# One VectorE maximum over two PSUM banks in every other burst of an attention kernel

## Chip, core and metric

The kernel runs on one core of one Trainium2 chip. The metric is the device time of one execution in microseconds (us); the time before is the median of three runs, 1784.49 us. Durations and waits come from one profiled execution of the kernel, which took 1784.4 us.

The engines named below are TensorE (PE in the profile; its weight loads are shown apart as PEld), VectorE (DVE), ScalarE (ACT), GpSimd (POOL) and SyncE (SP, which here only issues DMAs).

## What is computed

Two attention layers over one sequence (2048 rows, width 512, 32 heads of 16), mixed by a gate. Side A is full softmax attention. Side B is attention within four segments of 512 rows with a mask, plus a memory carried from segment to segment.

```python
def _A_ref(x, wqkv, wo):
    ...
    scores = jnp.einsum("bhqd,bhkd->bhqk", q, k) * scale
    p = _softmax(scores, axis=-1)
    o = jnp.einsum("bhqk,bhkd->bhqd", p, v)
    ...
def _B_ref(x, wq, wk, wv, wo, beta):
    ...
        logits = jnp.einsum("bhqd,bhkd->bhqk", qs, ks) * scale + mask
        p = _softmax(logits, axis=-1)
    ...
g = _sigmoid((x * gate_w).sum(-1, keepdims=True))
return g * a + (1 - g) * b
```

A softmax needs the maximum of each row of scores before the exponentials. The kernel takes these row maxima exactly, in a pass of its own, ahead of the scores whose exponentials it keeps. That pass is where the change lies.

## The kernel before

**Prologue** (about the first 300 us): projections of queries, keys and values for both sides, the memory of side B, and the maxima of the first 96 slots.

**Main loop.** The work is cut into 64 units: a side, a group of four heads, and a chunk of 512 query rows. A unit of side A has 64 slots, one of side B 10; a slot is one 512-column bank of scores. The loop `while n < nS or ...` (L1002 on) takes one score slot n and one maximum slot m = n + 96 per step, 2368 slots in all, so 2272 maximum slots (m from 96 to 2367) fall into the loop. The order of every queue is written out by hand: each engine executes its instructions in the order in which the loop emits them.

In one step the loop emits, in this order:

- `score_part(n)` (L726, L749): the score product on TensorE into one of three banks named `st`, then the exponential by ScalarE out of that bank into `p`.
- `max_part(m, ...)`: the product for the maxima on TensorE (L205, in `max_product`) into the bank `banks[m % 4]`, one of four PSUM banks of 512 fp32 columns named `sm0` to `sm3`; then VectorE takes the maxima of that bank. In a side-A slot this is one `tensor_reduce` of 512 columns (L226). In a side-B slot the bank holds one or two pieces (128 with 384 columns, 256 with 256, or one of 512), and each piece is a masked maximum (L238) and a short instruction that reads its accumulator. The first piece is emitted at once; a second piece waits in `rows_left` until `flush_rows()` in the next slot, after that slot's reduce.

Score products and maximum products alternate between the upper and the lower half of the array's rows, so the two of one slot run side by side.

A **burst** is three slots (`BURST = 3`). After the third slot of a burst the loop emits, on TensorE, one of three things: the products of the exponentials with the values (L783, `some_values`, 3 to 5 slots' worth, into the bank `ops`), or three products of the output projection (L895), or of a late query projection (L666). So TensorE's order in a burst is score, maximum, score, maximum, score, maximum, then this long block.

`maxs` lists whose maxima slot m takes. Slots of side B lie at m % 3 == 0, the first of a burst, so the second and third slot of a burst always belong to side A. When the last maximum of a unit is taken, `finish_max` reduces four key chunks to one (L183, VectorE), and the result travels through GpSimd, a transpose on TensorE and a DMA into rows of the query tile, 96 slots before the scores need it.

In the last 94 slots of scores no maxima remain; there the four banks serve the scores and the final products instead.

In the notes below M0 to M5 are the maximum products of six consecutive slots (m % 6 from 0 to 5), and R0 to R5 the reduces of these. A bank may be written again when the maximum out of it has ended: with four banks, product m waits for the reduce of slot m - 4.

Of the kernel before, what the change touches and what calls it, by code (L numbers as in the profile page):

```python
# [10 lines left out]
F32 = mybir.dt.float32  # L11
F32R = mybir.dt.float32r
AF = mybir.ActivationFunctionType
ALU = mybir.AluOpType
AX = mybir.AxisListType
# [7 lines left out]
CH = 512  # L23
# [24 lines left out]
def gated_mix(ctx, tc, x, xT, wqkv, a_wo, b_wq, b_wk, b_wv, b_wo, beta, gate_w, out):  # L48
    nc = tc.nc
# [129 lines left out]
    def finish_max(u):  # L179
        nm = pmt.pop(u)  # L180
        if u[0] == "A":
            pm, nm = nm, mp.tile([128, 4, 4], F32, tag="nm", name="nm")
            nc.vector.tensor_reduce(nm, pm, axis=AX.X, op=ALU.max, negate=True)  # L183

        ms = mp.tile([128, 2, 2, 2, 4], F32R, tag="ms", name="ms")
        nv = nm.rearrange("p (r h) s -> p r h s", r=2)
        nc.gpsimd.tensor_copy(ms[:, :, 0], nv)  # L187
        nc.gpsimd.tensor_sub(ms[:, :, 1], nv, ms[:, :, 0].bitcast(F32))
        return ms
# [14 lines left out]
    def max_product(ps, u, h, s, n0, n, k, k0=0):  # L204
        nc.tensor.matmul(ps[:, n0:n0 + n], rows(qt[u][:, :, s * 128:(s + 1) * 128], h, 48), rows(k[:, :, k0:k0 + n], h, 48),  # L205
                         start=True, stop=True)
# [3 lines left out]
    def flush_rows():  # L210
        while rows_left:
            rows_left.pop(0)()

    def max_part(m, bank):

        u, (r, i) = maxs[m]
        side, g, c = u
        if u not in pmt:
            pmt[u] = mp.tile([128, 4, 4] + [4] * (side == "A"), F32, tag="pm" + side, name="pm")
        pm = pmt[u]  # L220
        ps = bank()
        if side == "A":

            kc, s, h = i // 8, i % 8 // 2, 2 * r + i % 2
            max_product(ps, u, h, s, 0, CH, kt_[u, kc])
            nc.vector.tensor_reduce(pm[:, h, s, kc:kc + 1], ps, axis=AX.X, op=ALU.max)  # L226
            flush_rows()
        else:


            k = kt_[u, c]
            mine = [(2 * r + h, s, 128 * (s == 2) + 256 * (s == 1 and h), 128 * (s + 1))
                    for h, s in (((0, 0), (0, 2)), ((0, 1), (1, 1)), ((1, 0), (1, 2)), ((0, 3),), ((1, 3),))[i]]
            for h, s, n0, w in mine:
                max_product(ps, u, h, s, n0, w, k)
            flush_rows()
            for h, s, n0, w in mine:
                rows_left.append(lambda h=h, s=s, n0=n0, w=w: nc.vector.tensor_tensor_reduce(  # L238
                    out=tri["rest"][:, 0:w], in0=ps[:, n0:n0 + w], in1=tri["mask"][:, CH - w:], scale=-1.0, scalar=3.0e38,
                    op0=ALU.add, op1=ALU.min, accum_out=pm[:, h, s:s + 1]))  # L240
            rows_left.pop(0)()
        if m == last_max[u]:
            def finish():

                due = min(e for e in a_last if e >= last_max[u]) + LATE_T
                late.append((min(due, first[u] + LEAD - 12), u, finish_max(u)))
            todo.append((m + 1, finish))

    def run_todo(m):

        for e in [e for e in todo if e[0] <= m]:
            todo.remove(e)
            e[1]()

    def run_late(pool, tag, m):
        while us := [e for e in late if e[0] < m][:2]:
            for e in us:
                late.remove(e)
            transpose_max(us, pool, tag)
# [3 lines left out]
    def loads(m):  # L263

        m = min(m, len(maxs) - 1)
        while loaded[0] <= m:
            u, (r, i) = maxs[loaded[0]]
            if loaded[0] == first_max[u]:
                load_q(u)
            kc = u[2] if u[0] == "B" else i // 8  # L270
            if (u, kc) not in kt_:
                load_k(u, kc)
            loaded[0] += 1
# [3 lines left out]
    with ExitStack() as p0:  # L277
# [264 lines left out]
        def some_max():  # L542
            m = mnext[0]
            if m == LEAD:
                return
            loads(m + 3 + PRE)
            for i in range(4):
                max_part(m + i, lambda: me_sm.tile([128, CH], F32, tag="sm", name="sm"))
            run_todo(m + 3)
            mnext[0] += 4  # L550
            run_late(me_ps, "me", mnext[0])
# [51 lines left out]
    o_ps = ctx.enter_context(tc.tile_pool(name="o_ps", bufs=1, space=PSUM, reuse_waits="tile"))  # L603
    sm_ps = ctx.enter_context(tc.tile_pool(name="sm_ps", bufs=1, space=PSUM, reuse_waits="tile"))

    banks = [sm_ps.tile([128, CH], F32, name=f"sm{i}") for i in range(4)]

    ops = o_ps.tile([128, CH], F32, name="ops")

# [380 lines left out]
    def most():  # L990

        if not queue:
            return 0
        side = queue[0][1][0]
        left = SLOTS[side] - queue[0][2]
        over = 64 * (len(queue) - LOW) > (HIGH - LOW) * (left if side == "A" else 0)
        return ends[side].get(left, MOST + over)
# [3 lines left out]
    while n < nS or queue or beside or filled[0] < len(fill):  # L1001
        for f in beside.pop(n, []):  # L1002
            f()
        if n < nS:
            score_part(n)
        m = n + LEAD
        if m < nS:
            loads(m + PRE)

            max_part(m, lambda: banks[m % 4])  # L1010
        run_todo(m)
        if n >= nS or n % (2 * BURST if n in wide else BURST) == (2 * BURST if n in wide else BURST) - 1:
            taken = 0
            if shared:
                for _ in range(3):
                    shared.pop(0)()
            else:
                taken = some_values(n, 8 if n >= nS or n in wide else most())
            if n < 5:


                for i in range(4):
                    nc.tensor.matmul(ops[:, 128 * i:128 * i + 128], identf, identf, start=True, stop=True)
            if any(e[0] < m + 1 for e in late):
                run_late(st_ps, "st", m + 1)
            else:

                for _ in range(0 if n >= nS and queue else 4 if n not in wide else 11 - taken if taken < 8 else 0):
                    if filled[0] == len(fill) or fill[filled[0]][0] > n:
                        break  # L1030
                    fill[filled[0]][1]()
                    filled[0] += 1
        n += 1
# [18 lines left out]
def build():  # L1052
    import concourse.bacc as bacc
    nc = bacc.Bacc("TRN2", target_bir_lowering=False, num_devices=1)
    shapes = {"x": (S, D), "xT": (D, S), "wqkv": (D, 3 * D), "a_wo": (D, D), "b_wq": (D, D), "b_wk": (D, D),
              "b_wv": (D, D), "b_wo": (D, D), "beta": (H,), "gate_w": (D,)}
    args = [nc.dram_tensor(n, s, F32, kind="ExternalInput").ap() for n, s in shapes.items()]
    out = nc.dram_tensor("out", (S, D), F32, kind="ExternalOutput").ap()
    with tile.TileContext(nc) as tc:
        gated_mix(tc, *args, out)  # L1060
    return nc
# [23 lines left out]
```

## Time and profile before

| quantity | value |
|---|---|
| median of three runs | 1784.49 us (1784.37 to 1785.07) |
| the profiled execution | 1784.4 us |
| its span, first to last instruction | 1782.7 us |
| granted TensorE clock over the span | 1.000 |
| ScalarE busy | 1437.9 us, 81% of the span |
| GpSimd busy | 640.9 us, 36% of the span |

The profile's page gives, per engine, busy time and number of instructions, then the span in 40 slices, the DMA queues, the chain of work that ended last, and the costliest groups of instructions. A group's row reads: line, engine, operation, output tile and input tile, shapes, count, then busy time and mean duration of one. A row of the timeline reads: start in us, duration in us, engine, line, operation, tiles, shapes, count; in square brackets stands the idle time of the engine before it and what ended it. Two things matter in reading them. Matmuls are pipelined, so a busy TensorE row is not TensorE at its peak. And VectorE's durations overlap: the next instruction may start while the last one still drains, so the distance between starts is what an instruction costs when they follow closely.

### The profile page before, as it was taken

What the parts mean: (1) busy time and instruction counts of PE and PEld (TensorE: products, weight loads), DVE (VectorE), ACT (ScalarE), POOL (GpSimd) and SP (SyncE); (2) the same over time, 40 slices, a digit from 0 to 9 for tenths busy, and PEclk for the clock granted to TensorE, in tenths of its full rate; (3) what the DMA queues carried; (4) which work ended last, traced back from release to release, by engine and by line L of the source; (5) the groups of instructions that cost most, each with busy time, mean ns of one, the idle gap of its engine ahead of it and who ended that gap; (6) DMA issues with size and microseconds to landing.
All of it is one profiled execution on the core that took longest, in us unless ns stands there. A gap on an engine that the chain in (4) does not pass through costs nothing.

```text
span 1782.7 us, 40694 instructions
## 1 busy us (share of the span) xinstructions
PE 1773.5 (99%) x14945; PEld 912.4 (51%) x14945; DVE 1574.0 (88%) x3330; ACT 1437.9 (81%) x2754; POOL 640.9 (36%) x748
## 2 busy tenths in 40 slices
PE   9999999999999999999999999999999999999999
PEld 7887776444444444444444444444444444444444
DVE  4235777999999999999999999999999999999930
ACT  5455444888888888888888888888888888888884
POOL 3002222414161416443434343343434253435343
PEclk9999999999999999999999999999999999999999
DMA  7667555445463436544454544454545353544542
GB/s 227 219 226 249 189 195 192 132 103 140 108 169 107 134 116 180 147 136 135 134 134 128 146 127 146 128 146 115 157 106 156 115 142 116 147 119 140 144 161 61
DMA packets 142422, 261.55 MB, mean 147 GB/s; under 512 B 36328, under 2 KB 60680, under 8 KB 141712
## 3 DMA queue, kind: packets, MB, share of 16 engines
q1 hardware_dynamic: 140864, 257.69, 49.6%
q8 instruction: 119, 1.95, 0.5%
q0 software_dynamic: 1216, 1.14, 0.2%
q14 instruction: 79, 0.65, 0.1%
q10 hardware_dynamic: 144, 0.13, 0.0%
HBM read 174.39 MB, written 83.25 MB: 145 GB/s over the span
## 4 chain that ended last, share of the span: by engine, by line
PE 93%; DMA 2%; ACT 2%; DVE 1%; POOL 1%; issue 0%; SPq 0%; POOLq 0%; DVEq 0%; ACTq 0%
PE ops L783 33%; PE st L726 27%; PE sm L205 14%; PE pr L314 9%; PE ops L895 4%; PE ops L666 2%; PE sm L895 2%; DMA raw<-xT 1%; POOL mn L374 1%; PE num L496 1%; DMA qdA<-q 0%; DMA vs<-wqkv 0%; DMA qdB<-q 0%; DVE q L377 0%; ACT full L369 0%
## 5 line engine op out<-in xcount | busy, mean ns | idle before, releaser
L749 ACT ACTIVATE p<-st 128x512 f32<-128x512 f32 x2261 | 1189.4, 601 | 152.5 <-PE sm L205 108.6
L226 DVE TENSOR_REDUCE pm<-sm 128x1 f32<-128x512 f32 x2048 | 1280.8, 682 | 11.8 <-PE sm L205 11.6
L726 PE MATMUL st<-qA,kA 50*128 50x512 f32 x2014 | 663.1, 432 | 0.0
L205 PE MATMUL sm<-kA,qA 48*128 48x512 f32 x2048 | 658.9, 428 | 0.2
L783 PE MATMUL ops<-p,vA 128*17 128x128 f32 (+3 forms) x6432 | 551.9, 442 | 0.0
L726 PEld LDWEIGHTS st<-qA,kA 50*128 50x128 f32 x2014 | 327.5, 185 | 415.6 <-ACT p L749 371.0
L205 PEld LDWEIGHTS sm<-kA,qA 48*128 48x128 f32 x2048 | 330.6, 185 | 15.2 <-issue 6.4
L845 POOL TENSOR_TENSOR rcp<-rec,minus 128x32 f32<-128x32 f32 x43 | 234.2, 5446 | 76.3 <-DMA rec<-dend 71.7
L238 DVE CUSTOM_DVE_ANT_0 rest<-sm,mask 128x128 f32<-128x128 f32 (+3 forms) x512 | 247.3, 483 | 1.8 <-PE sm L205 0.3
L783 PEld LDWEIGHTS ops<-p,vA 128*17 128x17 f32 x6432 | 130.4, 96 | 214.7 <-issue 189.7
L730 POOL TENSOR_SCALAR_AFFINE_SELECT p<-p 128x512 f32<-128x512 f32 x128 | 79.4, 637 | 332.4 <-ACT p L749 327.9
L205 PE MATMUL sm<-kB,qB 48*128 48x128 f32 (+3 forms) x512 | 166.2, 384 | 0.0
L726 PE MATMUL st<-qB,kB 50*128 50x512 f32 (+1 forms) x495 | 109.4, 329 | 0.3 <-ACT mt L199 0.3
L377 DVE TENSOR_TENSOR q<-full,q 128x512 fp32r<-128x512 f32 x56 | 38.9, 694 | 70.2 <-ACT q L370 69.3
L726 PEld LDWEIGHTS st<-qB,kB 50*128 50x128 f32 x495 | 69.9, 186 | 59.3 <-ACT p L749 48.7
L783 PE MATMUL ops<-p,vB 128*17 128x128 f32 (+3 forms) x1504 | 87.5, 350 | 0.0
L205 PEld LDWEIGHTS sm<-kB,qB 48*128 48x128 f32 x512 | 79.9, 184 | 0.0
L187 POOL CAST ms<-nm 128x16 fp32r<-128x16 f32 x32 | 6.7, 208 | 203.1 <-DVE nm L183 201.3
L374 POOL TENSOR_SCALAR mn<-full 128x512 f32<-128x512 f32 x24 | 35.7, 1488 | 102.1 <-ACT full L369 81.7
L369 ACT COPY full<-pr 128x512 f32<-128x512 f32 x56 | 32.6, 582 | 39.3 <-PE pr L314 39.0
L187 POOL CAST ms<-pm 128x16 fp32r<-128x16 f32 x32 | 6.3, 196 | 128.5 <-DVE pm L238 128.4
L861 POOL TENSOR_TENSOR v<-v,inv 128x512 f32<-128x512 f32 x31 | 39.9, 1286 | 25.8 <-DMA inv<-rdA 22.1
(190 smaller groups left out, 1626.1 us busy)
## 6 DMA issues: line engine op xcount, KB each, us to landing
kA<-kdA SPq DMA_DIRECT2D x256, 128.0 KB
vA<-vdA SPq DMA_DIRECT2D x31, 544.0 KB
kA<-kdA SPq DMA_DIRECT2D x256, 64.0 KB
kdA<-q SPq DMA_DIRECT2D x32, 256.0 KB
qdB<-q SPq DMA_DIRECT2D x32, 256.0 KB
qA<-qdA SPq DMA_DIRECT2D x64, 128.0 KB
kdB<-q SPq DMA_DIRECT2D x32, 256.0 KB
qB<-qdB SPq DMA_DIRECT2D x64, 128.0 KB
```

The costliest lines, as they stand in the source:

```text
L205: nc.tensor.matmul(ps[:, n0:n0 + n], rows(qt[u][:, :, s * 128:(s + 1) * 128], h, 48), rows(k[:, :, k0:k0 + n], h, 48), start=True, stop=True)
L226: nc.vector.tensor_reduce(pm[:, h, s, kc:kc + 1], ps, axis=AX.X, op=ALU.max)
L238: rows_left.append(lambda h=h, s=s, n0=n0, w=w: nc.vector.tensor_tensor_reduce(out=tri["rest"][:, 0:w], in0=ps[:, n0:n0 + w], in1=tri["mas ...
L314: nc.tensor.matmul(ps, l(a, k), r(b, k), start=(n == 0), stop=(n == 11))
L374: nc.gpsimd.tensor_scalar_min(ph["mn"], full, 0.0)
L726: nc.tensor.matmul(ps[:, n0:n0 + CH - q0], rows(k[:, :, b * 128:(b + 1) * 128], h, 50), rows(q[:, :, q0:], h, 50), start=True, stop=True)
L730: nc.gpsimd.affine_select(out=x, in_=x, pattern=[[0, 4], [1, 128]], base=0, channel_multiplier=-1, compare_op=ALU.is_ge, fill=0.0)
L749: nc.scalar.activation(p[:, h], ps, AF.Exp, scale=SCALE)
L783: nc.tensor.matmul(ops[32 * h:32 * h + 17, q0:q0 + 128 * w], v[:, 17 * h:17 * h + 17], p[:, h, c0:c0 + 128 * w], start=(i == 0), stop=done ...
L845: eng.tensor_tensor(r, rec, minus, op=ALU.pow)
L861: eng.tensor_mul(k["v"], k["v"], k["inv"])
L895: yield lambda i=i, x=x, w=w: nc.tensor.matmul(ps, t[:, b, x], halved[side][:, o, w], start=start and i == 0, stop=stop and i == 2)
```

## The change

In the main loop, of every six slots the fifth and sixth (m % 6 == 4 and 5, the second and third slot of every other burst) no longer have a reduce each. The fifth emits only its product and notes in `half` where its result belongs. The sixth emits its product and then one `tensor_reduce` over both banks, [128, 2, 512] to two results per row, which are written with a stride into `pm`. For this the four banks become one tile `four` of four banks, and the bank of slot m is `banks[m % 4 ^ 1]`, so that the two results lie in rising order. `flush_rows()` is not called in the fifth slot; where the fourth slot is one of side B with two pieces, its second piece follows the double reduce. The prologue's calls pass no `two` and keep one reduce per bank.

```diff
-    def max_part(m, bank):
+    half = {}
+
+    def max_part(m, bank, two=None):
...
-            nc.vector.tensor_reduce(pm[:, h, s, kc:kc + 1], ps, axis=AX.X, op=ALU.max)
-            flush_rows()
+            to = 16 * h + 4 * s + kc
+            if two is not None and m % 6 == 4:
+                half[m] = u, to
+            elif m - 1 in half:
+
+                v, above = half.pop(m - 1)
+                assert v == u and to < above
+                nc.vector.tensor_reduce(pm.rearrange("p h s k -> p (h s k)")[:, to:above + 1:above - to],
+                                        two[:, m % 4 ^ 1:(m % 4 ^ 1) + 2], axis=AX.X, op=ALU.max)
+                flush_rows()
+            else:
+                nc.vector.tensor_reduce(pm[:, h, s, kc:kc + 1], ps, axis=AX.X, op=ALU.max)
+                flush_rows()
...
-    banks = [sm_ps.tile([128, CH], F32, name=f"sm{i}") for i in range(4)]
+    four = sm_ps.tile([128, 4, CH], F32, name="sm")
+    banks = [four[:, i] for i in range(4)]
...
-            max_part(m, lambda: banks[m % 4])
+            max_part(m, lambda: banks[m % 4 ^ 1], four)
```

## Prediction

> **What bounds the kernel now.** I read the page first (span, engines, chain), then the stages, then the instruction groups of a steady stretch, and last the timeline of a few bursts.
>
> ```profile
> span 1782.7 us, 40694 instructions
> PE 1773.5 (99%) x14945; PEld 912.4 (51%) x14945; DVE 1574.0 (88%) x3330; ACT 1437.9 (81%) x2754; POOL 640.9 (36%) x748
> PE ops L783 33%; PE st L726 27%; PE sm L205 14%; PE pr L314 9%; PE ops L895 4%; PE ops L666 2%; PE sm L895 2%; DMA raw<-xT 1%; POOL mn L374 1%; PE num L496 1%; DMA qdA<-q 0%; DMA vs<-wqkv 0%; DMA qdB<-q 0%; DVE q L377 0%; ACT full L369 0%
> ```
>
> The chain runs through TensorE, but 99% busy includes waiting inside the pipeline. The stage tells more:
>
> ```profile
> 700.00:1600.00 900.00, 899.96 (x8414) 414.78 (x8415) 898.54 (x1920) 796.38 (x1543) 364.76 (x410) 1.00 0.49 135
> ```
>
> In these 900 us VectorE (third pair) is busy 898.54 us: it is the full engine, with ScalarE at 796 us behind it. How full it really is comes from the distance of its starts. Groups of the same stretch, then four places of VectorE's timeline:
>
> ```profile
> L226 DVE TENSOR_REDUCE pm<-sm 128x1 f32<-128x512 f32 x1262 | 788.7, 682 | 0.1
> L238 DVE CUSTOM_DVE_ANT_0 rest<-sm,mask 128x512 f32<-128x512 f32 x80 | 54.7, 684 | 0.0
> L238 DVE CUSTOM_DVE_ANT_0 rest<-sm,mask 128x384 f32<-128x384 f32 x80 | 43.8, 547 | 0.0
> L238 DVE CUSTOM_DVE_ANT_0 rest<-sm,mask 128x256 f32<-128x256 f32 x80 | 33.2, 415 | 0.0
> L238 DVE CUSTOM_DVE_ANT_0 rest<-sm,mask 128x128 f32<-128x128 f32 x80 | 22.9, 287 | 1.3 <-PE sm L205 0.3
> L183 DVE TENSOR_REDUCE nm<-pm 128x16 f32<-128x64 f32 x19 | 3.9, 206 | 0.0
> ```
>
> ```profile
> 699.17 4.26 DVE L226 TENSOR_REDUCE pm<-sm 128x1 f32<-128x512 f32 x7
> ...
> 703.45 0.29 DVE L238 CUSTOM_DVE_ANT_0 rest<-sm,mask 128x128 f32<-128x128 f32 x1
> 703.66 0.08 DVE L238 DVE_READ_ACCUMULATOR2_ANT pm<- 128x1 f32 x1
> 703.66 0.69 DVE L226 TENSOR_REDUCE pm<-sm 128x1 f32<-128x512 f32 x1
> 704.26 0.55 DVE L238 CUSTOM_DVE_ANT_0 rest<-sm,mask 128x384 f32<-128x384 f32 x1
> 704.74 0.08 DVE L238 DVE_READ_ACCUMULATOR2_ANT pm<- 128x1 f32 x1
> ```
>
> Seven reduces take 4.26 us and one lasts 0.68, so starts lie (4.26 - 0.68) / 6 = 0.60 us apart. A masked piece takes 0.21 (128 columns) or 0.48 (384); a side-B slot of two pieces costs some 0.68, one of a single piece about a reduce. The stretch holds 1262 side-A slots and (3 x 80) / 2 + 80 = 200 of side B: 1462 slots, **6 slots in 900 / 1462 x 6 = 3.69 us**. VectorE's own need is 1262 x 0.60 + 120 x 0.68 + 80 x 0.61, about 888 us of 900. It waits little, 1 to 2%. TensorE is hardly looser:
>
> ```profile
> 695.95 0.40 PE L205 MATMUL sm<-kA,qA 48*128 48x512 f32 x1
> 696.28 1.06 PE L783 MATMUL ops<-p,vA 128*17 128x256 f32 x16
> 697.27 0.50 PE L726 MATMUL st<-qA,kA 50*128 50x512 f32 x1
> 697.27 0.73 PE L205 MATMUL sm<-kA,qA 48*128 48x512 f32 x2
> 697.61 0.62 PE L726 MATMUL st<-qA,kA 50*128 50x512 f32 x2
> 697.85 0.40 PE L205 MATMUL sm<-kA,qA 48*128 48x512 f32 x1
> 698.17 1.06 PE L783 MATMUL ops<-p,vA 128*17 128x256 f32 x16
> 699.16 0.50 PE L726 MATMUL st<-qA,kA 50*128 50x512 f32 x1
> 699.75 0.40 PE L205 MATMUL sm<-kA,qA 48*128 48x512 f32 x1
> 700.07 0.84 PE L783 MATMUL ops<-p,vA 128*17 128x256 f32 x16
> 700.85 0.50 PE L726 MATMUL st<-qA,kA 50*128 50x512 f32 x1
> ```
>
> ```profile
> 697.84 1.29 DVE L226 TENSOR_REDUCE pm<-sm 128x1 f32<-128x512 f32 x2
> ```
>
> A burst runs 0.58 us from its first maximum product to its third (697.27 to 697.85). Then comes the long block. Call V the time from a burst's third product to the next burst's first: 1.32 (695.95 to 697.27 and 697.85 to 699.16), 1.10 (699.75 to 700.85). A burst of 0.58 + 1.32 = 1.90 us is longer than three reduces (1.80); one of 1.68 is shorter. So each engine in turn waits for the other. The second fence shows how near: the first product of the burst starts at 697.27, lasts 0.50 like the score beside it, and its reduce starts at 697.84, 0.07 after that end: VectorE was waiting for it.
>
> **The change part by part.** In the loop, (2368 - 96) / 6 = 378 pairs of reduces become one instruction each.
>
> *What it removes.* Duration grows by (684 - 287) / 384 = 1.034 ns per column (the L238 rows). 512 columns are 0.53 us, so of the 0.60 us between starts 0.07 is paid per instruction. The double reduce then costs 1024 x 1.034 ns + 0.07 = 1.13 us between starts and lasts 0.68 + 0.53 = 1.21 us. No row shows a reduce over two banks. Bounds: the saving is 0 at worst (cost 1.20) and at best the whole fixed part of a reduce, 0.15 of its 0.68. The L183 reduce, with 16 results and 0.21 us, shows that several results in one instruction cost nothing visible, so I take 0.07. By itself: 378 x 0.07 = 26 us less VectorE work.
>
> The Trainium skill, "Perfetto Trace Analysis", section "Optimizing Scalar/DVE Operations", puts the overhead of a VectorE instruction on PSUM at about 125 ns and advises larger operations where the engine is saturated; by it the saving would be an estimated 378 x 0.125 = 47 us. The rows here show 0.07 instead. The same section says that where an engine causes bubbles on others without being saturated, breaking instructions up lets work complete sooner. Here both conditions hold at once, since VectorE and TensorE wait for each other.
>
> *What it adds: a later start and a later release.* The double reduce can start only when M5 has ended, and it holds two of four banks until it ends. Behind the release stand M2, the last product of the next burst (it needs the bank of slot 4), and M3, the first of the burst after (the bank of slot 5). M2 is emitted ahead of the long block, and TensorE goes in order: whatever M2 waits, the block and M3 wait too. What a release costs, from VectorE, PEld and PE rows of one such wait:
>
> ```profile
> 712.09 0.09 DVE L238 DVE_READ_ACCUMULATOR2_ANT pm<- 128x1 f32 x1
> ...
> 712.23 0.19 PEld L205 LDWEIGHTS sm<-kA,qA 48*128 48x128 f32 x2 [0.32 <-DVE pm L238]
> ...
> 712.23 0.51 PE L205 MATMUL sm<-kA,qA 48*128 48x512 f32 x2
> ```
>
> The maximum ends at 712.18, the weight load starts 0.05 later, the product ends 0.50 after the load began, 0.10 more than the 0.40 of a product that follows another. Now one cycle of six side-A slots, time 0 at the start of a double reduce:
>
> - it ends at 1.21; M2's load starts at 1.26;
> - M3 starts at 1.26 + 0.10 + V = 1.36 + V, with V of the first burst;
> - M3 ends 0.50 later and R3 starts 0.07 after that: 1.93 + V;
> - the next double reduce starts 0.60 after R3: **2.53 + V**. M5 is ready by then: M3 + 0.58 + 0.40 + 0.07 = M3 + 1.05, against M3 + 1.17.
>
> VectorE alone would need 1.13 + 4 x 0.60 = 3.53. TensorE alone would bring M2 0.58 + V after M5, that is at -0.59 + 0.58 + V, at most 1.31: before 1.36, so M2 does wait for the release. With V = 1.10 the cycle is 3.63, with V = 1.32 it is 3.85. Output products lie between:
>
> ```profile
> 718.23 0.39 PE L205 MATMUL sm<-kA,qA 48*128 48x512 f32 x1
> 718.55 0.97 PE L895 MATMUL ops<-wA,blk 128*128 128x512 f32 x3
> 719.44 0.50 PE L726 MATMUL st<-qA,kA 50*128 50x512 f32 x1
> ```
>
> V is 1.21 here. The mean over both kinds of burst is 900 / 1462 x 3 - 0.58 = 1.27; of the two blocks that follow a first burst in the rows above (695.95 and 699.75) the mean is 1.21. I take 1.21: **3.74 us** against 3.69.
>
> *Side B.* Where slot 3 is a two-piece slot, its first piece (0.21) ends before M5 is ready, so the double reduce starts M5-bound at about M3 + 1.10 instead of M3 + 1.17, 0.07 sooner; but the second piece, before the change hidden between R4 and R5, now stands behind the double reduce and ahead of R0. It takes 0.48, 0.34 or 0.48 (384 and 256 columns), 0.43 in the mean, and delays R3: 1.13 + 0.43 + 3 x 0.60 = 3.36, next start 3.96 instead of 3.74, and 0.08 later again when slot 0 is of side B too. Slots of side B lie on slots 0 and 3 about equally and three of five have two pieces: 320 x 3/5 / 2 = 96 such cycles, half with a neighbour in slot 0, each some 0.15 to 0.23 us longer. That is 96 x 0.19 = 18 us, 0.05 per cycle.
>
> *What is free.* `half`, the order of banks and the stride into `pm` issue no instruction and no DMA; the queues of SP and POOL keep their order. The finished maxima come up to a burst later; their cover is the 96 slots (some 59 us) before the scores need them.
>
> *Sum.* 3.74 + 0.05, and 0.01 for blocks that wait on copies out of `ops` as some do now: 3.80 against 3.69 per cycle, 378 x 0.11 = 41 us. The profiled execution took 1784.4 us (span 1782.7 and 1.7 around it), within 0.1 of the median. Forecast **1825 us**; its own range 1805 to 1848.
>
> **The rivals.**
>
> - *VectorE sets the pace throughout* (the other side). If M2's wait is absorbed, because V after the first burst is mostly 1.10 and side-B pieces fall into gaps, the cycle is 2.53 + 1.10 = 3.63, or 3.69 - 0.07 = 3.62: 378 x 0.07 = 26 us less, **1758**. For it: VectorE's 898.5 of 900. Against: V of 1.32 and 1.21 in the rows, and VectorE already waiting at 697.84. It decides where mean V is below 3.69 - 2.53 = 1.16.
> - *Gain and wait cancel*: V near 1.16 and side B hidden, cycle 3.69: **1784 to 1795**. The A-only sum is only 0.05 from this.
> - *The double reduce saves nothing* (1.20 us between starts, end at 1.28): each cycle 0.07 longer than the forecast, 26 us more, **1851**. Against: the straight line through the L238 rows.
> - *The change doesn't do what it says*: with one tile for four banks, products might be held by any maximum of the tile, not their own bank's. Then a slot costs a reduce and a refill in a row, 0.68 + 0.05 + 0.50 + 0.07 = 1.30 instead of 0.62, and the loop's 378 x 3.69 = 1395 us would grow by 1.1 times themselves: about **3300**. No row of this trace decides it.
>
> **How the numbers follow.** Forecast 0.70, VectorE's pace 0.12, cancelling 0.09, no saving 0.07, whole-tile waits 0.02. Range 1792 to 1852: it leaves out VectorE's pace, whole-tile waits and the lower edge of cancelling. What counts as no change is within 0.2%, 3.6 us. Faster 0.14, same 0.04, slower 0.82.
>
> **What would show it.** Right: 378 reduces of 1.21 us; a cycle of 3.8 us; VectorE idle about 0.1 to 0.3 us before R3, put down to PE sm; M2's weight loads waiting for VectorE. Wrong: VectorE still without gaps and cycles of 3.62 (then V was overestimated), or reduces of 1.28 us.

## The result and the profile after

After the change the kernel takes **4246.14 us** (six runs, 4241.1 to 4249.29) against 1784.78 (1784.2 to 1786.26) for the kernel before on the same chip: 2.3785 times as long, 95% interval 2.3754 to 2.3815. The profiled execution took 4244.9 us, 4243.2 of it the span. The forecast was 1825.

From the page of the kernel after: span, busy time of the engines, and the chain that ended last by line (line numbers after L205 are shifted: L741 is the score product, L798 the output product, L240 the single reduce, L236 the double one, L252 the masked piece).

```profile
span 4243.2 us, 40258 instructions
PE 3782.0 (89%) x14945; PEld 1553.5 (37%) x14945; DVE 1710.3 (40%) x2952; ACT 1550.4 (37%) x2754; POOL 639.3 (15%) x748
PE ops L798 26%; PE sm L205 24%; PE st L741 17%; DVE pm L240 14%; PE pr L328 4%; DVE rest L252 4%; PE ops L910 3%; PE ops L681 1%; PE sm L910 1%; ACT p L764 1%; PE sm L741 1%; POOL mn L388 0%; PE mt_ps L196 0%; PE num L510 0%; ACT ex L395 0%
```

VectorE is down from 88% to 40% of the span, although its work is all but the same: it is busy for 1710 us against 1574, since its instructions, which started 0.60 apart and lasted 0.68, now stand alone. New in the chain are VectorE's reduces (14%) and masked pieces (4%), and the maximum product is up from 14% to 24%: products and reduces now take turns. The windows of the loop, one stretch of 1000 us (busy time of PE, PEld, DVE, ACT, POOL, then the granted clock):

```profile
1000.00:2000.00 1000.00, 890.94 (x3466) 336.46 (x3465) 406.26 (x692) 356.85 (x636) 152.32 (x176) 0.51 0.19 51
```

Before, the stretch of 900 us had 8414 matrix products at a clock of 1.00; here 1000 us have 3466 at 0.51. "Busy" PE is no measure of work in such a loop. The groups of VectorE between 1000 and 3000 us:

```profile
L240 DVE TENSOR_REDUCE pm<-sm 128x1 f32<-128x512 f32 x639 | 442.0, 692 | 680.5 <-PE sm L205 628.4 <-PE st L741 52.1
L236 DVE TENSOR_REDUCE pm<-sm 128x2 f32<-128x1024 f32 x201 | 246.4, 1226 | 268.6 <-PE st L741 268.6
```

201 double reduces in 2000 us: **9.95 us for the cycle of six slots** that took 3.69. A single reduce is as long as before, within 0.01 us; ahead of each VectorE stands idle for 680.5 / 639 = 1.06 us in the mean, put down to a product. The timeline of the three engines shows the other half of this. VectorE, then weight loads, then one product:

```profile
2001.09 0.69 DVE L240 TENSOR_REDUCE pm<-sm 128x1 f32<-128x512 f32 x1 [0.91 <-PE sm L205]
2002.66 0.69 DVE L240 TENSOR_REDUCE pm<-sm 128x1 f32<-128x512 f32 x1 [0.89 <-PE sm L205]
2004.24 0.69 DVE L240 TENSOR_REDUCE pm<-sm 128x1 f32<-128x512 f32 x1 [0.88 <-PE sm L205]
```

```profile
2001.83 0.29 PEld L205 LDWEIGHTS sm<-kA,qA 48*128 48x128 f32 x1 [1.10 <-DVE pm L240]
...
2003.41 0.28 PEld L205 LDWEIGHTS sm<-kA,qA 48*128 48x128 f32 x1 [1.08 <-DVE pm L240]
```

```profile
2001.83 0.79 PE L205 MATMUL sm<-kA,qA 48*128 48x512 f32 x1 [0.38 <-DVE pm L240]
```

The reduce that starts at 2001.09 ends at 2001.78. The weight load of the next product waits for exactly that (1.10 us) and starts at 2001.83; the product ends at 2002.62, and its own reduce starts at 2002.66. So a slot is 0.69 of reduce, 0.05, 0.79 of product, 0.04: 1.57 us, in a row, with the other three banks standing unused. (Across the long block between two bursts the turn is longer.) Each product waits for the maximum of the slot just before it, in another bank, where before it waited for its own bank, four slots back.

The loop makes up (9.95 - 3.69) x 378 = some 2370 of the 2461 us. The rest lies behind the loop, as the first and fifth experiment show: from the last maximum to the end of the span the trace has 163.5 us, and 75.3 before the change.

### The profile page after: what moved, and what is told of

It is laid out like the page before. It is cut to its first block, busy times and chain, and to the rows that moved or that the text cites. A ratio compares the mean times of both kernels' runs of the same rounds, so it can differ in the third digit from the quotient of the medians.

```text
span 4243.2 us, 40258 instructions
## 1 busy us (share of the span) xinstructions
PE 3782.0 (89%) x14945; PEld 1553.5 (37%) x14945; DVE 1710.3 (40%) x2952; ACT 1550.4 (37%) x2754; POOL 639.3 (15%) x748
## 3 DMA queue, kind: packets, MB, share of 16 engines
q0 software_dynamic: 1216, 1.14, 0.1%
## 4 chain that ended last, share of the span: by engine, by line
PE 77%; DVE 18%; issue 2%; ACT 1%; DMA 1%; POOL 0%; SPq 0%; DVEq 0%; POOLq 0%; ACTq 0%
PE ops L798 26%; PE sm L205 24%; PE st L741 17%; DVE pm L240 14%; PE pr L328 4%; DVE rest L252 4%; PE ops L910 3%; PE ops L681 1%; PE sm L910 1%; ACT p L764 1%; PE sm L741 1%; POOL mn L388 0%; PE mt_ps L196 0%; PE num L510 0%; ACT ex L395 0%
## 5 line engine op out<-in xcount | busy, mean ns | idle before, releaser
L764 ACT ACTIVATE p<-st 128x512 f32<-128x512 f32 x2261 | 1276.9, 596 | 2181.2 <-PE st L741 1098.8
L205 PE MATMUL sm<-kA,qA 48*128 48x512 f32 x2048 | 1266.4, 771 | 411.9 <-DVE pm L240 271.9
L240 DVE TENSOR_REDUCE pm<-sm 128x1 f32<-128x512 f32 x1292 | 886.8, 691 | 1281.0 <-PE sm L205 1192.9
L741 PE MATMUL st<-qA,kA 50*128 50x512 f32 x2014 | 1244.7, 677 | 0.0
L798 PE MATMUL ops<-p,vA 128*17 128x128 f32 (+3 forms) x6432 | 978.8, 735 | 0.0
L205 PEld LDWEIGHTS sm<-kA,qA 48*128 48x128 f32 x2048 | 461.8, 279 | 1168.9 <-DVE pm L240 756.9
L741 PEld LDWEIGHTS st<-qA,kA 50*128 50x128 f32 x2014 | 573.2, 314 | 717.1 <-issue 683.9
L236 DVE TENSOR_REDUCE pm<-sm 128x2 f32<-128x1024 f32 x378 | 463.3, 1226 | 505.0 <-PE st L741 505.0
L252 DVE CUSTOM_DVE_ANT_0 rest<-sm,mask 128x128 f32<-128x128 f32 (+3 forms) x512 | 249.7, 488 | 463.3 <-PE sm L205 431.3
L798 PEld LDWEIGHTS ops<-p,vA 128*17 128x17 f32 x6432 | 168.4, 122 | 383.8 <-issue 366.2
L205 PE MATMUL sm<-kB,qB 48*128 48x128 f32 (+3 forms) x512 | 265.7, 593 | 0.0
L741 PE MATMUL st<-qB,kB 50*128 50x512 f32 (+1 forms) x495 | 191.0, 497 | 0.0
L741 PEld LDWEIGHTS st<-qB,kB 50*128 50x128 f32 x495 | 132.6, 318 | 120.4 <-issue 109.5
L798 PE MATMUL ops<-p,vB 128*17 128x128 f32 (+3 forms) x1504 | 155.4, 562 | 0.0
L205 PEld LDWEIGHTS sm<-kB,qB 48*128 48x128 f32 x512 | 131.4, 301 | 0.8 <-DVE pm L252 0.4
```

The lines of the kernel that those rows point to most:

```text
L236: nc.vector.tensor_reduce(pm.rearrange("p h s k -> p (h s k)")[:, to:above + 1:above - to], two[:, m % 4 ^ 1:(m % 4 ^ 1) + 2], axis=AX.X, ...
L741: nc.tensor.matmul(ps[:, n0:n0 + CH - q0], rows(k[:, :, b * 128:(b + 1) * 128], h, 50), rows(q[:, :, q0:], h, 50), start=True, stop=True)
L764: nc.scalar.activation(p[:, h], ps, AF.Exp, scale=SCALE)
L798: nc.tensor.matmul(ops[32 * h:32 * h + 17, q0:q0 + 128 * w], v[:, 17 * h:17 * h + 17], p[:, h, c0:c0 + 128 * w], start=(i == 0), stop=done ...
```

## The experiments

The theory was whole-tile waits: all four banks, being slices of one tile, are ordered as a whole between engines, so that a product waits for the last maximum of any bank. Its rivals were that the double reduce itself holds TensorE back so much, by keeping two banks, and that the drop of the clock is the larger part of the loss. Each time is compared with that of the kernel before on the same chip, 1784.4 to 1785.2 us; ratios stand with their 95% intervals.

### Only the waits are mended, and only the tile is merged

The first experiment is the kernel after, with every pair of instructions on different engines and different banks declared free of a dependence, in the main loop alone (maximum products, reduces, masked pieces; each against the last 24 of them, from the fifth experiment on the last 64). Here and below only the core of an edit is shown.

```diff
+    seen = []
+
+    def touch(ins, *on):
+        ins = ins.ins
+        for other, its in seen:
+            if not set(its) & set(on) and other.engine != ins.engine:
+                tc.declare_no_dep(ins, other, reason="other banks")
+        seen.append((ins, on))
...
-                nc.vector.tensor_reduce(pm.rearrange("p h s k -> p (h s k)")[:, to:above + 1:above - to],
+                i = nc.vector.tensor_reduce(pm.rearrange("p h s k -> p (h s k)")[:, to:above + 1:above - to],
...
+                touch(i, no, no + 1)
```

> The changed kernel, but each maximum product is held only by the maximum of its own bank, and each maximum only by the products of its own banks (378 double reduces as in the change). Theory W (the time of the changed kernel comes from products that wait for any maximum of the one tile, and from the lower granted clock that follows): the time falls back to that of the prediction's other steps, 1805 to 1848 us, granted clock 1.00, VectorE idle before R3, weight loads of M2 waiting for the double reduce. Rival V (once the waits are exact VectorE sets the pace and keeps the 0.07 us per pair): about 1758. Rival D (the double reduce itself is the trouble): far above 2000 still.

Measured: 1953.76 us, 1.0944 [1.0928, 1.0960]. Some 2290 of the 2461 us are gone with the double reduce still in place, so they came from the waits. The time is still above the 1805 to 1848 that was expected.

The second keeps the merged tile and never doubles a reduce; the third does this with the waits of the first.

```diff
-            max_part(m, lambda: banks[m % 4 ^ 1], four)
+            max_part(m, lambda: banks[m % 4 ^ 1])
```

> The kernel before with its four banks as one tile, and one reduce per bank as before: no double reduce. Theory W: each product waits for the maximum of the slot before it; per slot a product, a reduce and two hand-overs in a row, 6 of them in a cycle instead of 5: at least as slow as the changed kernel, 4250 to 4700 us, granted clock near 0.5. Rival D: 1784.

> One tile of four banks, one reduce per bank, waits held to the own bank: the control for e1. Theory W: 1784 within 5 us, since neither the tile nor the order of banks costs anything. If it differs from 1784, e1 is read against this run instead.

Measured: 4710.93 us, 2.6388 [2.6335, 2.6441], and 1871.33, 1.0478 [1.0460, 1.0495]. The tile alone, with not one double reduce, is worse than the whole change. Its loop has the same turn-taking, at the same clock. The window, then the turn across a long block:

```profile
1000.00:2000.00 1000.00, 861.74 (x3112) 323.54 (x3110) 375.70 (x703) 317.75 (x567) 128.95 (x151) 0.50 0.17 46
```

```profile
2003.66 0.79 PE L205 MATMUL sm<-kA,qA 48*128 48x512 f32 x1 [0.36 <-DVE pm L240]
2004.39 1.91 PE L798 MATMUL ops<-p,vA 128*17 128x512 f32 x8
...
2006.23 0.79 PE L205 MATMUL sm<-kB,qB 48*128 48x512 f32 x1
```

From one maximum product to the next, across the block, it takes 2.57 us here, where a turn inside a burst takes 1.57.

The double reduce even helps there: 4710.93 - 4246.14 is 1.23 us for each of 378 cycles, about what one of six turns less would give. So it is not the double reduce that makes the 2461 us. But the third lay far above the kernel before, with the same reduces as it; the waits were not all mended. Its trace says where: from the first maximum of the loop to the last it takes 1398 us, as the kernel before does (1399), and behind that 161 us instead of 75.

### Two tiles of two banks

```diff
-    four = sm_ps.tile([128, 4, CH], F32, name="sm")
-    banks = [four[:, i] for i in range(4)]
+    pair = [sm_ps.tile([128, 2, CH], F32, name=f"sm{i}") for i in range(2)]
+    banks = [pair[i // 2][:, i % 2] for i in range(4)]
```

The double reduce needs no more than this.

> The change with two tiles of two banks instead of one of four; double reduces as in the change. Theory W: a product of slot 1 waits for the reduce of slot 0 and that of slot 3 for that of slot 2, others for one two or more slots back; the wait of slot 3 is covered by the long block, that of slot 1 costs about 1.06 us per six slots: 378 x 1.0 us more, 2100 to 2300 us at full clock, more if the granted clock falls. Rival D: as slow as the changed kernel, 4250.

Measured: 2628.59 us, 1.4724 [1.4695, 1.4753], with the clock at 0.86:

```profile
1000.00:2000.00 1000.00, 899.13 (x6035) 389.29 (x6032) 677.50 (x1196) 607.13 (x1100) 254.06 (x287) 0.86 0.32 86
```

With two banks in a tile the loss is of the same kind and a third as large (844 of 2461 us). It is above the 2100 to 2300 us expected at full clock; the clock did fall.

### The waits of the last stage too

In the last 94 score slots there are no maxima left, and the four banks hold scores, closing products and their reads by ScalarE. The fifth experiment adds the declarations there; the sixth is the fifth with no reduce doubled, and so has the kernel before's instructions, only on a merged tile with exact waits.

```diff
+        own = 1 + n % BURST if n in wide and n // BURST % 2 else None
...
-            nc.scalar.activation(p[:, h], ps, AF.Exp, scale=SCALE)
+            i = nc.scalar.activation(p[:, h], ps, AF.Exp, scale=SCALE)
+            if own is not None:
+                touch(i, own)
```

> As e1_exact_waits, with the waits also held to the own bank in the last 94 score slots, where the four banks take scores and closing products. Theory W: the last stage returns to its length in the kernel before (some 85 us shorter than in e1), 1862 to 1872 us, granted clock above 0.99; the loop stays at 3.90 us per six slots. Rival T (the last stage was long for another reason): about 1954 as e1.

> One tile, one reduce per bank, exact waits everywhere: theory W 1784 within 5 us, so that the tile alone is without cost once the waits are exact, and e5 minus this run is the price of the double reduce. Rival T: about 1871 as e3.

Measured: 1871.59 us, 1.0487 [1.0471, 1.0502], and **1788.87, 1.0020 [1.0010, 1.0029]**. The sixth is the control of all that follows: merging the tile and changing the order of banks costs 3.7 us once the waits are exact. None of it lies in the loop, which takes 1398.7 us in both traces; from the last maximum to the end it is 79.1 us against 75.3. The last stage was worth 1953.76 - 1871.59 = 82 us with the double reduces and 1871.33 - 1788.87 = 82 without. Windows of that stage, first of the first experiment, then of the fifth:

```profile
1800.00:1954.00 154.00, 111.99 (x438) 47.83 (x436) 7.16 (x14) 49.61 (x92) 23.87 (x24) 0.69 0.16 51
```

```profile
1780.00:1870.00 90.00, 83.25 (x575) 43.26 (x575) 17.36 (x36) 58.10 (x117) 29.35 (x33) 0.98 0.31 102
```

438 products in 154 us, against 575 in 90.

With the waits out of the way the fifth is what the prediction described: the double reduce alone, 1871.59 - 1788.87 = **82.7 us** behind the control. Taken away in this order, the parts are: 4246.14 - 1953.76 = 2292 for the waits in the loop, 82 for those of the last stage, 82.7 for the double reduce and 3.7, together 2461. The windows of the same 900 us, fifth and then sixth:

```profile
700.00:1600.00 900.00, 892.56 (x8020) 419.56 (x8016) 861.89 (x1579) 759.39 (x1458) 358.36 (x403) 1.00 0.47 129
```

```profile
700.00:1600.00 900.00, 899.95 (x8414) 414.58 (x8414) 898.57 (x1921) 796.50 (x1543) 364.95 (x411) 1.00 0.49 135
```

In the control VectorE is as full as it was before the change (898.57 us against 898.54). With the double reduce it has gaps of 38 us, 0.16 in each of 231 cycles, and TensorE does 8020 products where it did 8414. The groups of the fifth in this stretch:

```profile
L255 DVE TENSOR_REDUCE pm<-sm 128x1 f32<-128x512 f32 x737 | 478.4, 685 | 18.5 <-PE sm L216 5.4 <-PE st L762 3.4
L250 DVE TENSOR_REDUCE pm<-sm 128x2 f32<-128x1024 f32 x231 | 281.7, 1219 | 4.8 <-PE sm L216 1.0
```

900 / 231 = 3.90 us per cycle; the prediction's sum was 3.80.

### More work for TensorE, to bring the clock back

What the clock alone costs was to be had by issuing each score product of the kernel after twice, and then four times (the repeats write the same result again).

```diff
-            nc.tensor.matmul(ps[:, n0:n0 + CH - q0], rows(k[:, :, b * 128:(b + 1) * 128], h, 50),
-                             rows(q[:, :, q0:], h, 50), start=True, stop=True)
+            for _ in range(2):
+                nc.tensor.matmul(ps[:, n0:n0 + CH - q0], rows(k[:, :, b * 128:(b + 1) * 128], h, 50),
+                                 rows(q[:, :, q0:], h, 50), start=True, stop=True)
```

> The changed kernel with every score product of the main loop issued twice into its bank (more TensorE work, same result). Theory C (a good part of the 4246 us is the granted clock of 0.51, which falls because TensorE pauses in every slot): the clock rises towards 1 and the time falls although there is more work, to 3100 to 3500 us; at full clock six slots in a row need about 7.4 us. Rival: the clock does not react to it, and the time is 4250 us or more.

> The changed kernel with every score product of the main loop issued four times. With two (e7) TensorE still paused in every slot and its clock stayed at 0.55. Theory C: with four the pauses are filled at half clock, the granted clock rises to 0.9 or more, and then three extra products (0.24 us each) fit into the 0.7 us of a reduce: 3100 to 3600 us. Rival: the clock stays near 0.55 and the extra products lengthen every slot: 5500 us or more.

Measured: 4570.09 and 5192.77 us, one run each. Both missed their purpose. Windows of the loop, twice and then four times:

```profile
1000.00:2000.00 1000.00, 933.28 (x3815) 423.37 (x3813) 373.93 (x631) 329.42 (x583) 137.83 (x162) 0.54 0.18 47
```

```profile
1000.00:4000.00 3000.00, 2871.29 (x12978) 1652.26 (x12978) 971.29 (x1648) 867.13 (x1519) 352.75 (x404) 0.61 0.15 40
```

The clock stayed at 0.54 and 0.61, so neither run shows the turn-taking at full clock, and how much of the 2370 us is the clock's own share stays open. An estimate from the prediction's whole-tile chain, which reckons at full clock: 3300 us, where the second run took 4711 and 82 of them lie in the last stage, so some 1300 of that run's 2926 us would be the clock's.

### The double reduce in some pairs only

Where do the 82.7 us come from? Three kernels with the fifth's waits double only some of the 378 pairs: the 96 in which slot 3 is a side-B slot of two pieces, and of the others the 104 that are followed by a short block (V of 1.07 in the mean of the trace before) and the 148 followed by a long one (1.31). The 30 pairs between short and long weren't run alone. The edit, with another constant in each:

```diff
-            if two is not None and m % 6 == 4:
+            if two is not None and m % 6 == 4 and PAIRS >> (m - 100) // 6 & 1:
```

> As e5, with a double reduce only in the 104 cycles whose following first burst has a short block (V of 0.88 to 1.10, mean 1.05) and whose slot 3 is not a two-piece slot of side B; one reduce per bank elsewhere. Theory V (a cycle costs 2.53 + V, at least what VectorE needs): 104 x 0.07 less than 1784, about 1777, or no change. Rival P (each pair costs the same, e5 minus e6 over 378): 104 x 0.217 = 23 more, 1807.

> As e5, with a double reduce only in the 148 cycles whose following first burst has a long block (V about 1.30) and whose slot 3 is not a two-piece slot of side B. Theory V (2.53 + V per cycle): 148 x 0.14 = 21 us over e6, about 1810. Rival P (the same price for each pair, 0.12 as in e8): 18 over, 1807; with the 0.22 of the mean 32 over, 1821.

> As e5, with a double reduce only in the 96 cycles whose slot 3 is a two-piece slot of side B. By the prediction's step (0.15 to 0.23 each) 18 us over e6, about 1807. If what e8 leaves of e5's 83 us lies here, 96 x 0.4 = 40 us over e6, about 1829.

| pairs doubled | time, us | ratio [95%] | over the kernel before, less the control's 3.7 | per pair |
|---|---|---|---|---|
| 104 short | 1801.45 | 1.0089 [1.0074, 1.0104] | 12.6 | 0.12 |
| 148 long | 1822.95 | 1.0217 [1.0202, 1.0232] | 34.9 | 0.24 |
| 96 side B | 1838.20 | 1.0300 [1.0283, 1.0317] | 50.1 | 0.52 |

No set gains, not even the short one, for which 1777 was expected, and the side-B set lost more than either figure expected of it. The three come to 97.6 us, more than the 82.7 of all pairs together. The traces show why. Counted on VectorE from the start of one slot 3's maximum to that of the next, and set against the control, the doubled cycles themselves lose 3.8, 28.4 and 46.3 us, nearly what the same cycles lose in the fifth (4.9, 29.3 and 45.7). Another 7.8, 5.7 and 3.8 us lie in the cycles right behind them, which in the fifth are doubled themselves. So the price per pair in the table contains the cycle behind it, most of all in the short set. The mechanism in a cycle of the long set, on VectorE, PEld and PE:

```profile
885.24 1.22 DVE L252 TENSOR_REDUCE pm<-sm 128x2 f32<-128x1024 f32 x1
...
888.49 0.69 DVE L272 CUSTOM_DVE_ANT_0 rest<-sm,mask 128x512 f32<-128x512 f32 x1
...
889.11 1.22 DVE L252 TENSOR_REDUCE pm<-sm 128x2 f32<-128x1024 f32 x1
```

```profile
886.51 0.18 PEld L218 LDWEIGHTS sm<-kA,qA 48*128 48x128 f32 x1
```

```profile
887.93 0.50 PE L218 MATMUL sm<-kB,qB 48*128 48x512 f32 x1
```

The double reduce ends at 886.46, M2's load follows at 886.51 (1.27 after the start), M3 starts 1.42 later at 887.93, its maximum 0.56 after that at 888.49, the next double reduce 0.62 later: 3.87 us.

The side-B set lost most, and its trace shows what else waits. VectorE, then PEld:

```profile
910.41 0.28 DVE L272 CUSTOM_DVE_ANT_0 rest<-sm,mask 128x128 f32<-128x128 f32 x1
...
910.81 1.23 DVE L252 TENSOR_REDUCE pm<-sm 128x2 f32<-128x1024 f32 x1
911.95 0.55 DVE L272 CUSTOM_DVE_ANT_0 rest<-sm,mask 128x384 f32<-128x384 f32 x1
912.42 0.08 DVE L272 DVE_READ_ACCUMULATOR2_ANT pm<- 128x1 f32 x1
```

```profile
912.56 0.19 PEld L218 LDWEIGHTS sm<-kA,qA 48*128 48x128 f32 x2 [0.79 <-DVE pm L272]
```

Both pieces of slot 3 lie in one bank. The first is read at 910.41, the second only behind the double reduce, at 911.95, and its result is out at 912.50. That bank is the one of the next burst's second product, whose load stands 0.79 us for it; in TensorE's order everything behind that product stands too.

### The second piece ahead of the double reduce

If that is so, the remedy is to take the second piece while the fifth slot's reduce would have run, before the double one:

```diff
             if two is not None and m % 6 == 4:
                 half[m] = u, to
+                flush_rows()
```

> As e11 (double reduces in the 96 cycles with a two-piece slot 3), but the second piece of side B is emitted in slot 4, ahead of the double reduce, where VectorE waits for the product of slot 5. Theory B (in e11 the second product of the next burst waits for that late piece, 0.5 us each): nearly all of e11's 49 us over e6 goes, 1785 to 1797 us; a gain over the kernel before of up to 96 x 0.07 = 7 us can be seen only if it comes below 1781. Rival: the price lies in the hold of the two banks as in e10 (0.23 each), 1811.

> As e5 (all 378 double reduces, exact waits), the second piece ahead of the double reduce. Theory B: e5 less the 0.5 us of 96 cycles, plus what the other cycles cost (e8 and e10: 13 + 34, and some 5 for the 29 between): 1830 to 1845 us. Rival: 1865 to 1872 as e5.

Measured: 1813.55 us with the 96 pairs, 1.0162 [1.0147, 1.0177], and 1843.94 with all 378, 1.0332 [1.0315, 1.0349]. Less the control's 3.7 these lie 25.1 and 55.5 us above the kernel before. VectorE, with the 96 pairs:

```profile
906.61 0.41 DVE L273 CUSTOM_DVE_ANT_0 rest<-sm,mask 128x256 f32<-128x256 f32 x1
...
907.07 0.43 DVE L273 CUSTOM_DVE_ANT_0 rest<-sm,mask 128x256 f32<-128x256 f32 x1
...
907.42 1.22 DVE L253 TENSOR_REDUCE pm<-sm 128x2 f32<-128x1024 f32 x1
```

and PE in the burst behind it:

```profile
908.17 0.73 PE L218 MATMUL sm<-kA,qA 48*128 48x512 f32 x2
```

The pieces follow each other, the double reduce starts behind them without a pause, and the next burst's first two products run together. Half the loss of the side-B pairs is gone (50.1 to 25.1), and 82.7 - 55.5 = 27 us of the whole. With the 96 pairs 1785 to 1797 was expected; what stays, 0.26 us a pair, is near what the rival gave for the hold of the two banks (1811). Of all pairs, 55 us remain with every second piece out of the way. No version tried is faster than the kernel before.

## Why the forecast failed

**What bounds the kernel.** Right: VectorE full and TensorE hardly looser. The control shows the same 899 us of 900.

**The double reduce.** Right: 1.21 us long was the estimate, 1.219 is measured; 1.13 between starts, 1.14 measured (910.81 to 911.95). One instruction less is worth 0.06 to 0.07 us.

**The chain from its end to the next one.** Right in every link of the cycle shown: 1.26 to M2's load (1.27), 0.10 + V to M3 (1.42 in a long block, where V of 1.32 was given), 0.57 to the reduce (0.56), 0.60 to the next double one (0.62). The medians over the 148 long cycles of the fifth are 1.27, 1.42, 0.56 and 0.61.

**What is free.** Here is the step that failed. "`half`, the order of banks and the stride into `pm` issue no instruction and no DMA" is true. But the one tile that took the place of four was left out of this list, and so its waits were put at nothing in the sum. It stood only among the rivals, at a chance of 0.02 because no row decided it. The runs decided it: 4710.93 us with the tile and no double reduce, 1788.87 with the tile and exact waits. That rival had the mechanism, and its chain was right in all links but one (0.68 + 0.05 + 0.50 + 0.07; measured 0.69, 0.05, 0.79, 0.04); its price of 3300 was short for two reasons. It reckoned at full clock, and the clock fell to 0.51: the product takes 0.79 and the long block up to 1.91, so that every third turn takes longer still (2.57 in the rows of the second experiment). And it left out the last 94 slots, which use the same banks for other things, and which cost 82 us more.

**The sum of the forecast.** With exact waits it is 41 us against 82.7, on the right side and half of it. V was right, by luck: 1.21 was taken from two blocks, and the mean behind all first bursts of the trace before is 1.21 too. Cycle by cycle, counted as above and with the mean V of each kind in 2.53 + V (for side B the side-B step, 3.74 + 0.19; the last of the 378 pairs has no cycle behind it):

| cycles | control, us | by the forecast | fifth, us | loss in all, us |
|---|---|---|---|---|
| 104 short | 3.65 | 3.60 | 3.70 | 4.9 |
| 148 long | 3.68 | 3.84 | 3.88 | 29.3 |
| 96 side B | 3.75 | 3.93 | 4.23 | 45.7 |
| 29 between | 3.72 | 3.77 | 3.81 | 2.5 |

The largest term that was mis-sized is side B, and one more was too small:

- *Side B*, 4.23 us where 3.93 was reckoned, which is 29 us in 96 cycles: the delay of VectorE was counted, but not that the late second piece keeps slot 3's bank from the next burst's second product. With the second piece ahead of the double reduce these cycles take 3.93, though not by the forecast's reckoning, which had the piece behind.
- *The hold of two banks*: 55 us are measured with the second pieces ahead, so whatever that order costs is in it, where the forecast had 23 (0.06 a cycle). The long cycles are within 0.04 of the chain. The short ones, which by the chain should have gained 5 us, lost 5. In the control TensorE is ahead there: the maximum of slot 3 starts 0.80 us after its product does (median), where the chain needs 0.57; in the fifth it is 0.61. So the double reduce used up a lead that a mean V doesn't show. That the cycle behind a short one loses for want of this lead (7.8 us when only the short ones are doubled) is argued; no run isolates it.

**The rivals.** VectorE's pace (1758) and the cancelling were out: V alone doesn't set the cycle. "The double reduce saves nothing" (1851) is nearer to the 1871.59 with exact waits than the forecast is, but not by its reason: the instruction did save its 0.07.

## What to carry to other kernels

A change of how buffers are declared is a change of waits: when separate buffers become slices of one, find out for each engine what it will be ordered against, in every stage that uses them, before the saving is counted. A saved fixed cost of 0.07 us per instruction did not pay here, where two engines are both full and the longer instruction keeps two of four buffers. Where an instruction grows, look for short leftover work that it now delays and that still holds a buffer, and put that ahead of it.

## What was unexpected of the hardware

The granted clock of TensorE fell from 1.00 to 0.51 for a whole loop whose pauses are short. From the waits of the kernel after, between 1000 and 3000 us (in total, times, longest):

```profile
PE sm L205 <- DVE pm L240: 145.8, 388, 0.5
PE sm L205 <- DVE pm L252: 66.4, 119, 1.0
```

These are all but the whole of TensorE's pauses, 11% of the 2000 us, and none is over 1.0 us, yet the clock stays down. The trace's records of the clock know only full and half: here mostly some 365 us at half and then 3.4 at full. With two tiles the records swing, 57 stretches at full and 57 at half, and the mean in the loop is 0.86.

The Trainium skill, "TensorE: Matmul & The Clock Gate", section "HAM oscillation — how this bites in real kernels", sums up its rule as no TensorE gaps over some 3.4 us; by that these gaps should have cost no clock, and the measurement differs. The Trainium skill, "TensorE: Matmul & The Clock Gate", section "A second HAM failure mode: psum-queue depth-cycling", also tells of a kernel whose frequent micro-idles while cycling through banks make the clock swing; the run with two tiles fits that, and the changed kernel stays down rather than swings. What share of busy time would keep the clock up is open: two and four times the score products brought 0.54 and 0.61.
